# Token rows in SBUF at a pitch of 264 bytes instead of 256, in a long convolution by FFT with a token-mixing layer behind it

## The chip, the cores and the metric

The kernel runs on one core of a Trainium2 chip. The metric is the device time of one execution in microseconds. A profile comes from one execution; its times count from the first instruction of the program. Engines are called PE (matrix products; PEld is its loading of weights), DVE (vector), ACT (activation), POOL (general purpose, and the issuer of some DMAs) and SP (issuer of the other DMAs).

## What is computed

The input x has 8 batches of 5696 tokens with 128 channels. The first part convolves every channel of x with a filter h along the tokens, by FFT of double length; the second mixes tokens and channels.

```python
def _attn_ref(x, h):
    B, S, D = x.shape          # 8, 5696, 128
    L = 2 * S
    Xf = np.fft.rfft(x, n=L, axis=1)
    Hf = np.fft.rfft(h, n=L, axis=0)
    Yf = Xf * Hf[None, :, :]
    return np.fft.irfft(Yf, n=L, axis=1)[:, :S, :]

def _moe_ref(x, w_theta, w_tok_r, w_tok_i, w_ch):   # x: the result above
    theta = x @ w_theta
    zr, zi = x * np.cos(theta), x * np.sin(theta)
    y = einsum('ts,bsd->btd', w_tok_r, zr) + einsum('ts,bsd->btd', w_tok_i, zi)
    u = x + y
    return u + np.maximum(u @ w_ch, 0.0)
```

## The kernel before

**The FFT as matrix products.** The double length of 11392 is split as N1 x N2 = 178 x 64. A token number is 64 m + n, so the 5696 tokens are 89 rows m (NB = 89, on 89 partitions) of 64 columns n (N2). The forward transform has two stages, then comes the product with the transform of h, and two stages lead back:

- Stage A (`stage_a`, line 194) transforms along m. For one channel, the 89 x 128 block of x (two batches e, 64 columns n) is loaded into PE as weights, and the table f1_t (89 x 180: cosines and sines of 90 frequencies) is moved over it. Four channels make one chunk, which fills a PSUM tile and is emptied into the tile a (line 201, on ACT). A group has 64 channels, so 16 chunks.
- Stage B (`stage_b`, with `f2`, line 212) transforms along n, copies the result to SBUF (line 310, ACT) and multiplies it twice with tiles hs of the filter's transform (line 312, DVE) into u_t and v_t. hs is read from HBM by SP in 12 chunks per group, four chunks ahead.
- Stage C (`stage_c`, lines 328 and 329) and stage D (`stage_d`, line 351) transform back. C has 16 chunks of 16 matmuls; most of its results are emptied by DVE (line 336), some by ACT (lines 333, 334).

**Groups and their order.** There are eight groups: four pairs of batches (bp) times two halves of the channels (dh). PE takes its instructions in program order. In the loop at line 602, stage C of group g is woven with stage A of group g+1 (stage A first; it takes the first 0.35 of the stretch when g has the first half, 0.55 when it has the second), then stage B of group g+1 with stage D of group g. For the first group stage A runs alone (line 380).

**The loads of x.** `load_x` brings a pair of batches into the tile x16 of 128 x 2 x 64 x 128 float16 values, of which 89 partitions are used. The values are float32 in HBM and are converted by the DMA; such DMAs are issued by POOL. One load has 16 DMAs: two batches, four runs of 16 columns n, and partitions 0 to 79 and 80 to 88 apart. Within a partition a DMA's 16 columns of 128 channels lie in one run both in HBM (8 KB) and in SBUF (4 KB). The tile has one buffer, so the load of the next pair starts when the stage A that reads the second half is through (`next_x`, line 612, put at the end of that stage A's list). At most eight of these DMAs are under way at once; the ninth waits on the first.

The weights of one matmul in stage A are `x16[:NB, :, dh * HD + q]` with e and n merged: 128 columns at a step of one row of x16. The filter's own stage A, before all groups, reads `h16` in the same way, with rows of 64 values.

**What stands beside the loads.** POOL also makes the tables of sines and cosines (`turns_of`: an IOTA at line 150 and a product at line 152, then DVE at lines 155 and 156, then ACT); f2 needs the table w_t2 from there. The first x load is issued among these instructions. After the eight groups x16's room is given up and the mixing part follows: weights of 5696 x 5696 come in through a ring of buffers (line 509, POOL, converted from float32 by the DMA), are transposed by DVE (line 714) and multiplied on PE (line 1099).

Of the kernel before, what the change touches and what calls it, by code (L numbers as in the profile page):

```python
# [12 lines left out]
F16 = mybir.dt.float16  # L13
# [9 lines left out]
def kernel(  # L23
# [11 lines left out]
    B, S, D = x.shape  # L35
    assert D == 128
    P = 128
# [39 lines left out]
    N2 = 64  # L77
# [4 lines left out]
    HD = D // 2  # L82
    EN = N2 // 2 + 1
    WARM = 12
    assert N1 * N2 == NF and NB * N2 == S and NB % 2 == 1 and K1 <= P
    CHK = [(c0, min(CK, K1 - c0)) for c0 in range(0, K1, CK)]
    NCK = len(CHK)
# [14 lines left out]
    def pool(name, bufs, stack, **kw):  # L102
        return stack.enter_context(tc.tile_pool(name=name, bufs=bufs, **kw))
# [3 lines left out]
    fx = pool("fft_x", 1, xin)  # L107
# [11 lines left out]
    for p0, p1 in ((0, 80), (80, NB)):  # L119
        nc.gpsimd.dma_start(u_t[p0:p1, :N2 * D],  # L120
                            bass.AP(tensor=h.tensor, offset=h.offset + p0 * N2 * D,
                                    ap=[[N2 * D, p1 - p0], [1, N2 * D]]))

    def load_x(bp):
        x16 = fx.tile([P, 2, N2, D], F16, tag="x16", name="x16")
        for e in range(2):
            src = x[2 * bp + e]
            for n0 in range(0, N2, 16):
                for p0, p1 in ((0, 80), (80, NB)):
                    nc.gpsimd.dma_start(  # L130
                        x16[p0:p1, e, n0:n0 + 16, :].rearrange("p n d -> p (n d)"),
                        bass.AP(tensor=src.tensor, offset=src.offset + (p0 * N2 + n0) * D,
                                ap=[[N2 * D, p1 - p0], [1, 16 * D]]))
        return x16

    lane = fc.tile([P, 2], F32)
# [67 lines left out]
    def f2(a_st, c):  # L204
# [11 lines left out]
        if c == NCK - 1:  # L216
            for n in range(WARM):
                nc.tensor.matmul(ps[:, n % 2, ck * HD:ck * HD + 384], w_t2[:, 2, :P],
# [11 lines left out]
    for k0 in (0, 15, 30):  # L230
        w_table(k0)
    nc.vector.tensor_copy(h16[:NB], u_t[:NB, :N2 * D].rearrange("p (n h d) -> p h n d", h=2, d=HD))
    x16s = {0: load_x(0)}
    steps, a_h = stage_a(lambda q: h16[:NB].rearrange("p h n d -> p (h n) d")[:, :, q], True)
    woven(steps, [lambda k0=k0: w_table(k0) for k0 in range(45, K1, 15)])
# [366 lines left out]
    for g, (bp, dh) in enumerate(groups):  # L602
        st = {}
        last = g + 1 == len(groups)
        a_, load_, b_ = front(g + 1)
        if last:
            for _ in range(3):
                steps0.pop(0)()
        now = [with_load(steps0.pop(0), n < 6) for n in range(9)] if last else []
        c_ = stage_c(st, last)  # L610
        if dh == 0 and bp + 1 < B // 2:
            def next_x(bp=bp):
                x16s[bp + 1] = load_x(bp + 1)
            a_ = a_ + [next_x]
        woven((c_, 0.06 if a_ else 0.0, 1.0), (a_, 0.0, 0.35 if dh == 0 else 0.55), now, load_)
        if g + 2 == len(groups):
            xin.close()
            open_phases()
            load_ya0()
        now = [steps0.pop(0) for _ in range(5)] if last else []  # L620
        woven(b_, (stage_d(st, bp, dh, load_ya1 if last else None), 0.0, 1.1 if b_ else 1.0), now)
        if g + 2 == len(groups):
            load_ya1()
            open_ring()
# [537 lines left out]
```

## Time and profile before

| | us |
|---|---|
| three runs | 2100.75, 2101.3, 2103.45 |
| median | 2101.3 |
| span of the profiled execution, first to last instruction | 2098.1 |
| first matmul of stage A with x as weights | 54.5 |
| last one | 358.4 |
| the 512 matmuls of stage A: busy time on PE | 77.2 |
| mean of one of their weight loads | 0.241 |
| the four x loads begin (first issue on POOL) | 5.0, 100.0, 184.8, 270.1 |
| they have landed | 36.7, 118.3, 202.6, 289.6 |
| the stage A that needs them begins | 54.5, 128.8, 214.3, 301.0 |

The profile gives no time of its own for the profiled execution besides the span; the median of the runs is 3.2 us longer than the span.

How to read the lines that follow. In the list of costliest groups a line has the source line, the engine, the operation, what it writes and reads, shapes, the count, then busy time in us and mean of one in ns, then idle time before these instructions and what ended it. In the timeline a line has start and length in us, the engine, line and operation, and in brackets the idle time before it; several instructions in a row are merged (x12). In the DMA view a queue's line has packets, MB and the time that its packets took as a share of the 16 DMA engines; q0 carries what POOL issues, q1 what SP issues. The share can go over 100%, since a packet's time can overlap the next one's. In the 40 slices of the page each digit is the busy share in tenths, and PEclk the granted clock of PE in tenths of full speed. PE's matmuls are pipelined, so that their recorded lengths overlap; the distance between starts is the pace.

### The profile page before, as it was taken

The page shows a single profiled execution, that of the slowest core. Times are in us where ns is not written, and L with a number is a line of the kernel's source. Part 1 is how long each engine was busy: PE and PEld are TensorE (multiplying, and loading weights), DVE is VectorE, ACT ScalarE, POOL GpSimd, SP SyncE. Part 2 cuts the span into 40 slices and gives each one's busy share as a digit, 9 for nine tenths or more (in the row PEclk, how much of TensorE's full clock was granted, in tenths as well). Part 3 has the DMA queues.
Part 4 walks back from the last instruction along what each step waited for, and adds up shares of the span by engine and source line. Part 5 has one row for each costly group of instructions (what it writes and reads, how often), then busy time and mean ns, then how long its engine had stood idle before and what let it go on. Part 6 is the DMA issues. An engine that isn't in the chain of part 4 may idle for free.

```text
span 2098.1 us, 41505 instructions
## 1 busy us (share of the span) xinstructions
PE 1979.5 (94%) x15688; PEld 1109.4 (53%) x15865; DVE 1595.2 (76%) x2881; ACT 675.3 (32%) x995; POOL 912.5 (43%) x1662
## 2 busy tenths in 40 slices
PE   4888999878999999999999999899999999999998
PEld 3788888754444444444444444344444444444444
DVE  7777776776878888888886766886777777777867
ACT  5887877874332333333310000011111111111111
POOL 5301010327444636354557554435354545445450
PEclk8799999989999999999999999999999999999999
DMA  7357474989989989898999989869797887879693
GB/s 144 94 137 175 123 171 121 239 243 239 179 153 179 178 175 168 171 173 177 171 175 152 154 167 284 136 107 156 127 154 132 148 142 136 154 130 155 126 155 89
DMA packets 408233, 334.97 MB, mean 160 GB/s; under 512 B 85895, under 2 KB 358407, under 8 KB 407047
## 3 DMA queue, kind: packets, MB, share of 16 engines
q0 software_dynamic: 225952, 156.72, 52.8%
q1 hardware_dynamic: 176096, 164.05, 27.3%
q10 hardware_dynamic: 5984, 11.54, 1.6%
q8 instruction: 124, 2.03, 0.4%
q14 instruction: 77, 0.63, 0.1%
HBM read 377.11 MB, written 92.49 MB: 224 GB/s over the span
## 4 chain that ended last, share of the span: by engine, by line
PE 63%; DVE 4%; DMA 2%; issue 2%; POOL 0%; ACT 0%; DVEq 0%
PE m L1099 59%; DVE c L1106 2%; DMA ring<-in_moe_w_tok_r_dram 1%; DVE b L655 1%; PE v L801 1%; PE utp L794 1%; PE m L1103 1%; DVE wt L714 1%; PE tpz L742 0%; PE theta_ps L396 0%; POOL ring L509 0%; PE m L986 0%; DMA yT<-yt_hbm 0%; PE m L1020 0%; DMA zl<-zl_hbm 0%
## 5 line engine op out<-in xcount | busy, mean ns | idle before, releaser
L509 POOL DMA_DIRECT2D ring<-in_moe_w_tok_i_dram x720 | 390.8, 557 | 653.0 <-DVE wt L714 579.6
L509 POOL DMA_DIRECT2D ring<-in_moe_w_tok_r_dram x720 | 389.0, 559 | 145.8 <-DVE wt L714 85.5
L714 DVE STREAM_TRANSPOSE wt<-ring 128x384 f32<-128x384 f32 (+2 forms) x720 | 359.3, 523 | 110.3 <-PE m L1099 70.0
L1099 PE MATMUL m<-b,wt 128*128 128x512 bf16 x1599 | 385.9, 380 | 4.1 <-DVE wt L714 1.7
L1099 PEld LDWEIGHTS <-wt 128*128 128x128 bf16 x1804 | 176.4, 98 | 219.7 <-DVE wt L714 7.8
L1106 DVE TENSOR_TENSOR c<-c,m 128x512 f32<-128x512 f32 x412 | 265.2, 669 | 0.4 <-PE m L1099 0.4
L796 ACT ACTIVATE ring<-utp 128x512 bf16<-128x512 bf16 x85 | 50.8, 597 | 582.3 <-PE utp L794 582.3
L328 PE MATMUL ps<-r_u,u_t 128*128 128x128 f16 x1024 | 126.4, 223 | 6.4 <-ACT red L419 3.0
L329 PE MATMUL ps<-r_v,v_t 128*128 128x128 f16 x1024 | 125.5, 223 | 0.4
L1020 PE MATMUL m<-b,wt 128*128 128x512 bf16 x466 | 110.2, 381 | 8.9 <-DMA b<-z_hbm 4.9
L791 ACT ACTIVATE ub<-c 128x512 bf16<-128x512 f32 x88 | 55.0, 628 | 191.5 <-DMA ring<-in_moe_w_tok_r_dram 113.0
L130 POOL DMA_DIRECT2D x<-in_x_dram x64 | 33.9, 536 | 184.9 <-PE ps L194 174.8
L328 PEld LDWEIGHTS <-u_t 128*128 128x128 f16 x1024 | 103.4, 101 | 5.5 <-DVE u_t L312 4.6
L329 PEld LDWEIGHTS <-v_t 128*128 128x128 f16 x1024 | 102.4, 100 | 4.4 <-issue 2.4
L310 ACT ACTIVATE xs<-ps 128x1024 f16<-128x1024 f32 x96 | 96.6, 1030 | 14.7 <-DVE v_t L312 6.7
L312 DVE TENSOR_TENSOR u_t<-xs,hs 128x1024 f16<-128x1024 f16 x96 | 68.6, 715 | 29.2 <-ACT xs L310 19.0
L1020 PEld LDWEIGHTS <-wt 128*128 128x128 bf16 x528 | 51.1, 99 | 69.2 <-issue 9.6
L194 PE MATMUL ps<-f_t,x 89*128 89x180 f16 x512 | 77.2, 298 | 4.0 <-ACT xs L310 2.6
L212 PEld LDWEIGHTS <-w_t 64*128 64x128 f16 x3240 | 60.8, 102 | 37.5 <-issue 24.5
L398 ACT ACTIVATE red<-theta_ps,magic 128x512 f32<-128x512 f32 (+1 forms) x46 | 31.6, 687 | 134.6 <-PE theta_ps L396 104.5
L194 PEld LDWEIGHTS <-x 89*128 89x128 f16 x512 | 70.8, 241 | 5.5 <-issue 4.5
L744 ACT ACTIVATE ring<-tpz 128x512 bf16<-128x512 bf16 (+1 forms) x46 | 27.5, 597 | 131.9 <-PE tpz L742 113.0
(2895 smaller groups left out, 3868.9 us busy)
## 6 DMA issues: line engine op xcount, KB each, us to landing
ring<-in_moe_w_tok_r_dram POOLq DMA_DIRECT2D x352, 96.0 KB, 4.5
ring<-in_moe_w_tok_i_dram POOLq DMA_DIRECT2D x352, 96.0 KB, 4.9
ring<-in_moe_w_tok_r_dram POOLq DMA_DIRECT2D x352, 80.0 KB, 4.5
ring<-in_moe_w_tok_i_dram POOLq DMA_DIRECT2D x352, 80.0 KB, 3.9
hs<-hf_hbm SPq DMA_DIRECT2D x192, 128.0 KB, 3.1
cp_hbm<-c SPq DMA_DIRECT2D x88, 256.0 KB, 2.5
c<-cp_hbm SPq DMA_DIRECT2D x88, 256.0 KB, 4.4
out_dram<-c SPq DMA_DIRECT2D x88, 256.0 KB, 4.5
```

The source lines that it names most:

```text
L194: nc.tensor.matmul(ps[:, i // 2, (i % 2) * 2 * K1:(i % 2 + 1) * 2 * K1], lhs(q + i), f1_t[:NB], start=True, stop=True)
L212: nc.tensor.matmul(ps[:, e, j * HD:(j + 1) * HD], w_t2[rows, c0 + j, N2 * (1 - ri):N2 * (3 - ri)], a_st["a"][rows, ri * K1 + c0 + j, :], s ...
L310: nc.scalar.activation(xs[:, :, :, :ck], ps, AF.Copy)
L312: nc.vector.tensor_tensor(uv[r][:, :, :, c0:c0 + ck], xs[:, :, :, :ck], hv[:, r:r + 1, :, :ck].to_broadcast([P, 2, HD, ck]), op=mult)
L328: nc.tensor.matmul(o, u_t[:, at:at + P], r_u, start=True, stop=False)
L329: nc.tensor.matmul(o, v_t[:, at:at + P], r_v, start=False, stop=True)
L509: nc.gpsimd.dma_start(wb[32 * i:32 * i + 32, :ng, :nj * 64], bass.AP(tensor=a.tensor, offset=a.offset + row0 * S + p * H + i * QR + j0 * 6 ...
L714: nc.vector.transpose(wt.rearrange("p j t r -> p (j t r)").bitcast(F32).rearrange("p (j g t) -> p g j t", j=TJ, g=4)[:, :ng, :nj], wb[:, : ...
L791: nc.scalar.activation(ub[:m].rearrange("p b d -> p (b d)"), c[:m], AF.Copy)
L1020: nc.tensor.matmul(ms[n // 2 * 2 + h], a[n][:, j, :, r], bts_of[p][jj][n % 2 * 2 + h][:, r, :], start=(n % 2 == 0 and jj == 0 and r == 0), ...
L1099: nc.tensor.matmul(ms[q], a[q][:, j, :, r], bts[jj][q][:, r, :], start=(jj == 0 and r == 0), stop=(jj == NJ - 1 and r == 1 and q not in left))
L1106: nc.vector.tensor_tensor(c, z, ms[q], op=op)
```

## The change

The rows of x16 get a pitch XP = D + 4 = 132 values (264 bytes) instead of 128 (256 bytes); the four values at the end of each row are neither written nor read. The loads name the 128 values of each row, so the SBUF side of a DMA is no longer one run per partition, and the HBM side is written with the row as a dimension of its own. What is moved, and all matmuls, stay as they are; only the step between the columns of stage A's weights differs. The tile takes 33,792 bytes per partition instead of 32,768.

```diff
     WARM = 12
+    XP = D + 4
...
     def load_x(bp):
-        x16 = fx.tile([P, 2, N2, D], F16, tag="x16", name="x16")
+        x16 = fx.tile([P, 2, N2, XP], F16, tag="x16", name="x16")
         for e in range(2):
             src = x[2 * bp + e]
             for n0 in range(0, N2, 16):
                 for p0, p1 in ((0, 80), (80, NB)):
                     nc.gpsimd.dma_start(
-                        x16[p0:p1, e, n0:n0 + 16, :].rearrange("p n d -> p (n d)"),
+                        x16[p0:p1, e, n0:n0 + 16, :D],
                         bass.AP(tensor=src.tensor, offset=src.offset + (p0 * N2 + n0) * D,
-                                ap=[[N2 * D, p1 - p0], [1, 16 * D]]))
+                                ap=[[N2 * D, p1 - p0], [D, 16], [1, D]]))
         return x16
```

## The prediction

> **What bounds the kernel.** I read the page's engine table first, then its 40 slices, then the chain. PE is busy for 94% of the span and the chain lies on PE for 63% of it, almost all of that in a line of the later mixing part; the change touches only the first 360 us.
>
> ```profile
> PE 1979.5 (94%) x15688; PEld 1109.4 (53%) x15865; DVE 1595.2 (76%) x2881; ACT 675.3 (32%) x995; POOL 912.5 (43%) x1662
> ...
> PEclk8799999989999999999999999999999999999999
> DMA  7357474989989989898999989869797887879693
> ...
> L194 PE MATMUL ps<-f_t,x 89*128 89x180 f16 x512 | 77.2, 298 | 4.0 <-ACT xs L310 2.6
> ```
>
> The stages follow one another on PE in program order, so I count a microsecond won or lost before 360 us as one at the end. The last line, from the costliest groups, shows where: stage A, 512 matmuls with x as weights, fills 77 us of PE.
>
> **The intended gain: the weight read.** Stage A against its neighbour, stage C, in the timeline:
>
> ```profile
> 131.42 0.22 PE L328 MATMUL ps<-r_u,u_t 128*128 128x128 f16 x1
> 131.48 0.22 PE L329 MATMUL ps<-r_v,v_t 128*128 128x128 f16 x1
> ```
> ```profile
> 92.97 1.57 PEld L194 LDWEIGHTS <-x 89*128 89x128 f16 x12
> ```
>
> Stage C, 128 columns moved over contiguous weights, starts a matmul every 0.055 us. By columns stage A's 180 would take 0.055 x 180/128 = 77 ns. But its twelve weight loads took 1.57 us, the last of them about 0.24 (the page's mean), so 1.33/11 = 121 ns from start to start. So at full clock stage A is paced by its weight loads, 44 ns over its matmul. At half clock a matmul needs twice 77 ns and nothing is to be won.
>
> Whether 264 bytes read faster than 256 no row shows. The nearest are loads in stretches at half clock (from 88.8 to 92.0 us, and h from 16 to 19):
>
> ```profile
> L194 PEld LDWEIGHTS <-x 89*128 89x128 f16 x10 | 1.5, 207 | 0.0
> L328 PEld LDWEIGHTS <-u_t 128*128 128x128 f16 x9 | 1.3, 140 | 0.0
> ```
> ```profile
> L194 PEld LDWEIGHTS <-h 89*128 89x128 f16 x21 | 3.2, 172 | 0.0
> ```
>
> Contiguous weights (u_t) take 140 ns, h16 with a column step of 128 bytes 172, x16 with 256 bytes 207. So the step matters. Two readings fit: farther steps simply cost more (then 264 costs what 256 does), or powers of two return to the same part of the memory (then 8 bytes more may help a little or much). By nearness 264 is next to 256, and 8 bytes leave neighbouring columns almost where they were modulo 256. I take **no gain**, and keep both ends. Upper end of the gain: group 0's stage A gives nothing, since ACT empties PSUM back to back there (16 evictions in 10.79 us, 0.67 each, against 4 x 0.121 = 0.48 on PE). For the other 448 matmuls, some 85% of which the timeline has at full clock, 44 ns is 448 x 0.044 x 0.85 = 16.8 us, 2.4 per group; ACT's idle time before these evictions was only 1.7 to 2.3 us per group, so I count 1.9 x 7 = **13 us**. Lower end: if the longer step cost as much again as that from 128 to 256 bytes, 35 ns, it would be 448 x 0.035 x 0.85 = 13 us of loss.
>
> The Trainium skill ("SBUF — State Buffer", Specifications (TRN2)) says that full bandwidth needs two accesses or more to a 16-byte line and that each crossing to a new line pays. By it 128, 256 and 264 bytes are all the same, since every column is a new line, and the gain is nothing. The rows agree that strided weights are slower, but not that all strides are equal (172 against 207).
>
> **The price: the loads of x.** One x load is 16 DMAs (eight of 80 partitions, eight of 9), issued by POOL, which convert from float32. Today a partition's 16 rows are one run of 4 KB in SBUF. With gaps of 8 bytes they become 16 runs of 256 bytes: 712 pieces per load become 712 x 16 = 11,392. On this queue pieces of converting DMAs are not joined: the weight ring's 768- and 640-byte rows appear one packet each. Rates, from the DMA view of four stretches (packets, MB, share of 16 engines): 102 to 114 us (x), 1050 to 1052 (640-byte rows), and the two kinds of 1053 to 1058 (128-byte rows beside other traffic):
>
> ```profile
> q0 software_dynamic: 836, 2.39, 104.1%
> ```
> ```profile
> q0 software_dynamic: 665, 0.38, 133.3%
> ```
> ```profile
> q0 software_dynamic: 1595, 0.21, 63.3%
> q1 hardware_dynamic: 806, 0.72, 50.8%
> ```
>
> Now: 836 packets less 252 that only signal are 584 in 12 us, so 712 take 14.6 us. The 640-byte rows: 665 less 73 are 592 in 2 us on 16 engines, 54 ns each. The 128-byte rows: 0.633 x 5 x 16 / 1595 = 31.7 ns, over a total share of 1.14, so 28 ns of service. A 256-byte piece lies a quarter of the way: 28 + 26/4 = **34 ns** (ends: 28 and 54). A load is then 11,392 x 34/16 = 24.2 us instead of 14.6 (ends: 19.9 and 38.5).
>
> Is there room? The x16 buffer is single, so a load starts when the second half's stage A has read it, and must land before the next pair's stage A:
>
> ```profile
> 100.00 4.25 POOL L130 DMA_DIRECT2D x<-in_x_dram  x8 [27.41 <-PE ps L194]
> ```
> ```profile
> 128.76 1.94 PE L194 MATMUL ps<-f_t,x 89*128 89x180 f16 x12
> ```
> ```profile
> q0 software_dynamic: 1024, 2.92, 54.5%
> q1 hardware_dynamic: 1345, 2.21, 27.4%
> q8 instruction: 5, 0.08, 1.1%
> ```
>
> The window is 100.0 to 128.7; the last of x lands at 118.3 today (issues and landings of the timeline), 10.4 us early. The last fence is the DMA view of this window: besides x the engines carry 27.4% of 28.7 = 7.9 us of hs (the filter tiles) and 0.3 of instructions. After a lead-in of some 1.3 us they have 27.4 us; they would need 24.2 + 7.9 + 0.3 = 32.4. So x is **5.0 us late**, and PE, which takes its instructions in order, stands before stage A with stage C's matmuls queued behind. The 0.7 us or so of landing and the half microsecond that PE idles there now (0.36 before the first C matmul) cancel. The windows of the loads at 184.8 and 270.1 are alike (landings at 202.6 and 289.6 before matmuls at 214.3 and 301.0): 3 x 5 = 15 us. Which loses, x or hs, matters little: late hs holds DVE's multiplication, which comes before the same point.
>
> POOL's own part: the 512-piece DMAs of line 542 took 802 ns, the 80-piece ones 531, so 271/432 = 0.63 ns per piece and 1200 x 0.63 = 0.75 us more per large DMA. For the later loads it is covered: 8 x 1.28 + 8 x 0.56 = 14.7 us of issue beside 24 us of transfer. In the first load it stands ahead of the tables:
>
> ```profile
> 23.03 6.16 POOL L130 DMA_DIRECT2D x<-in_x_dram  x11
> 29.19 1.97 POOL L150 IOTA whole<- 128x960 f32 x2
> 31.26 2.22 POOL L152 TENSOR_SCALAR turn<-whole,lane 128x960 f32<-128x960 f32 x2
> ```
>
> Six large ones from 21 us on move this by 4.5 us; the first of the two L152 then ends at 36.9 instead of 32.4, and DVE, which took it at 35.86, is **1.0 us** late, with the tables for which PE waits. The two large ones before fall into POOL's wait of 9.42 us at 20.10. The first load's transfer (landed by 36.7, needed at 54.5) has 18 us of room and needs 10 more. One KB more of SBUF per partition costs no time.
>
> The Trainium skill ("DMA: Bandwidth & Descriptors", Why small descriptors are slow) gives a 256-byte piece 8 data cycles and 3 of overhead. By that estimate a load would take 14.6 x 11/8 = 20.1 us, nearly in time, and the change would cost 2 to 4 us. The rows above (a fifth of the bytes for half the time) say more.
>
> **Sum.** 1.0 + 15 + 0 = +16 us on a span of 2098.1. The page gives no other time for the profiled execution; the median of the runs, 2101.3, lies 3.2 above its span, and I add the same: 2098.1 + 16 + 3.2 = 2117.3.
>
> **Rivals.**
> 1. *The read becomes fast and x still lands in time* (piece near 28 ns, or a better spread over the engines): -13 + 1 = -12, 2089. For: 172 against 207 at half and whole step, and 10.4 us of slack today. Against: both must hold. It decides from a piece below 28 ns.
> 2. *Fast read, late x*: -13 + 16 = +3, 2104 (2092 to 2115).
> 3. *The pitch does not do what it says and x lands in time*: +1 to +3, 2103.
> 4. *The read gets slower*: +13 + 16, 2130.
>
> **Numbers.** Chances: forecast 0.42, rivals 0.16, 0.18, 0.17, 0.07. Forecast's own range: 1 + 3 x 0.7 gives 2104 at 28 ns a piece, and 45 ns (32.0 us a load, 12.8 late) gives 2141; 54 ns would be 2160. The range from 2092 to 2141 leaves out most of rival 1 and the far ends. By 0.2% (4.2 us, about what a measurement can tell from no change): faster is rival 1 and a quarter of 2, 0.21; the same is most of 3, half of 2 and the forecast's lowest end, 0.25; slower is the rest, 0.54.
>
> **What would show it.** Right: about 46,000 packets more on q0; stage A's weight loads still near 121 ns apart and 207 long at half clock; x landing 130 to 135 us instead of 118, with PE idle before L194 on the DMA of x three times; the L130 issues near 1.3 us. Wrong: weight loads under 90 ns apart, joined packets on q0 (then no lateness at all), or x landing before 128 us.

## The result, and the profile after

The changed kernel takes 2090.7 us (median of four runs, 2088.3 to 2092.4) against 2101.2 for the kernel before, run beside it: a ratio of 0.9946, interval 0.9931 to 0.9960. It is 11 us faster, where I had forecast 16 us slower. The profiled execution took 2088.3 us with a span of 2086.5 (before: 2098.1).

The engine table and two rows of the 40 slices, of the changed kernel:

```profile
PE 1968.8 (94%) x15865; PEld 1085.1 (52%) x15865; DVE 1579.1 (76%) x2881; ACT 659.4 (32%) x995; POOL 915.7 (44%) x1662
...
PEclk8799989999999999999999999999999999999999
DMA  9489595989898989898999899869697878878793
```

PE still carries the span, with 11 us less of busy time. The granted clock shows one thing that I had not asked about: the sixth slice, 261 to 313 us, has 8 here and 9 before. The cause comes below.

**The weight read became fast.** The view of stage A's line, before and then after (min/median/max in ns, first and last start in us, the shape):

```profile
L194 PEld LDWEIGHTS <-x x512: 202/238/310, 54.2 to 358.2; 89*128 89x128 f16 x171
L194 PE MATMUL ps<-f_t,x x512: 237/292/406, 54.5 to 358.4; 89*128 89x180 f16 x171
```
```profile
L195 PEld LDWEIGHTS <-x x512: 149/157/188, 56.8 to 347.9; 89*128 89x128 f16 x171
L195 PE MATMUL ps<-f_t,x x512: 237/241/359, 56.9 to 348.0; 89*128 89x180 f16 x171
```

The median weight load fell from 238 to 157 ns. What counts is the pace, read from the timeline as in the prediction:

```profile
91.94 1.01 PEld L195 LDWEIGHTS <-x 89*128 89x128 f16 x12
```

Twelve loads in 1.01 us, the last of them about 0.157: (1.01 - 0.157)/11 = 78 ns from start to start, where it was 121. That is the 77 ns that the 180 columns need, so weight loads no longer pace stage A.

**The pieces came as forecast, and moved faster.** The DMA view from the issue of the second x load to the stage A that needs it (97.9 to 130.1 us):

```profile
q0 software_dynamic: 12544, 2.92, 95.4%
q1 hardware_dynamic: 1351, 2.22, 26.9%
q8 instruction: 5, 0.08, 1.0%
```

The load is 12,544 packets instead of 1024, for the same 2.92 MB. Its last piece lands at 123.05 us, 7 us ahead of the need:

```profile
97.92 7.56 POOL L131 DMA_DIRECT2D x<-in_x_dram  x10 [24.58 <-PE ps L195]
```
```profile
130.13 1.14 PE L195 MATMUL ps<-f_t,x 89*128 89x180 f16 x12
```

**Where the time went.** A period is the time from one group's stage A to the next one's. The loads of x fall between groups 1 and 2, 3 and 4, 5 and 6. All in us, from the first matmuls of stage A in the traces:

| | before | changed |
|---|---|---|
| stage A of group 0 begins | 54.5 | 56.9 |
| period from group 0 | 30.0 | 29.4 |
| periods with an x load (from groups 1, 3, 5) | 44.2, 45.2, 46.2 | 43.8, 46.7, 47.8 |
| periods without (from groups 2, 4, 6) | 40.3, 40.5, 40.1 | 36.9, 36.5, 36.5 |
| stage A of group 7 | 17.3 | 13.6 |

A period without an x load keeps a gain of 3.4 to 4.0 us. One with a load keeps 0.4 or loses 1.5, although its stage A is just as much shorter (first to last matmul: 14.9, 15.1, 14.7 before, 11.1, 11.2, 11.3 after). All eight stages A together became 25.6 us shorter. The pieces took back 2.4 at the start and, in the three periods, 3.4, 5.4 and 5.0 us of what stage A had won, 13.8 in all. That makes -9 of the -11.6 in the span; the rest lies scattered in the other periods and behind stage A. The experiments first price the two halves and then ask how pieces that land in time can cost that much.

### The profile page after: what moved, and what is told of

The parts are those of the page before. It is cut to its first block, busy times and chain, and to the rows that moved or that the text cites. A ratio compares the mean times of both kernels' runs of the same rounds, so it can differ in the third digit from the quotient of the medians.

```text
span 2086.5 us, 41684 instructions
## 1 busy us (share of the span) xinstructions
PE 1968.8 (94%) x15865; PEld 1085.1 (52%) x15865; DVE 1579.1 (76%) x2881; ACT 659.4 (32%) x995; POOL 915.7 (44%) x1662
## 4 chain that ended last, share of the span: by engine, by line
PE 64%; DVE 3%; DMA 3%; issue 1%; POOL 1%; ACT 0%; DVEq 0%; POOLq 0%
PE m L1100 60%; DMA ring<-in_moe_w_tok_r_dram 2%; DVE c L1107 1%; POOL ring L510 1%; PE v L802 1%; PE utp L795 1%; PE m L1104 1%; DVE b L656 1%; DVE wt L715 1%; PE theta_ps L397 0%; PE tpz L743 0%; PE m L987 0%; PE m L1021 0%; DMA ring<-in_moe_w_tok_i_dram 0%; DMA zl<-zl_hbm 0%
## 5 line engine op out<-in xcount | busy, mean ns | idle before, releaser
L131 POOL DMA_DIRECT2D x<-in_x_dram x64 | 48.5, 764 | 169.1 <-PE ps L195 159.5
L311 ACT ACTIVATE xs<-ps 128x1024 f16<-128x1024 f32 x96 | 91.8, 984 | 19.4 <-PE ps L213 5.2
L421 ACT ACTIVATE mag<-mag,half_pi 128x512 f32<-128x512 f32 (+1 forms) x90 | 65.6, 729 | 0.0
L313 DVE TENSOR_TENSOR v_t<-xs,hs 128x1024 f16<-128x1024 f16 x96 | 63.5, 662 | 0.0
```

Source lines behind the costliest of these rows:

```text
L311: nc.scalar.activation(xs[:, :, :, :ck], ps, AF.Copy)
L313: nc.vector.tensor_tensor(uv[r][:, :, :, c0:c0 + ck], xs[:, :, :, :ck], hv[:, r:r + 1, :, :ck].to_broadcast([P, 2, HD, ck]), op=mult)
L421: nc.scalar.activation(mag, mag, AF.Sin, bias=half_pi[:m], scale=-TWO_PI)
```

## The experiments

All times are compared with the kernel before, run beside each one.

### The pieces alone: pitch 128, each DMA takes every fourth row

```diff
-    x16[p0:p1, e, n0:n0 + 16, :].rearrange("p n d -> p (n d)"),
+    x16[:, e].rearrange("p (k j) d -> p j k d", j=4)[p0:p1, n0 // 16],
...
-            ap=[[N2 * D, p1 - p0], [1, 16 * D]]))
+            ap=[[N2 * D, p1 - p0], [4 * D, 16], [1, D]]))
```

> The pitch stays at 128 values, but each DMA of the load takes every fourth row, so that its runs in SBUF are 256 bytes long as in the changed kernel: the small pieces without the new column step. Theory (the change is a gain of about 25 us in stage A, less about 14 us in the three stretches in which x is loaded and 2 us at the start): 2115 to 2118 us, weight loads as before (about 240 ns), the periods that hold an x load 4 to 5 us longer than before, the others as before. Rival (the small pieces cost nearly nothing, and the rest of stage A's gain is lost because ACT or DVE become the bound of the weave): 2101 to 2104 us.

Measured: 2119.5 us against 2101.7, ratio 1.0088 (1.0073 to 1.0103). The pieces alone cost 18 us, a little more than I had expected. The three periods with a load take 51.1, 51.5 and 51.5 us; those without stay at 40.

### The pitch alone: rows of 132 values, filled as unbroken runs

```diff
-    x16[p0:p1, e, n0:n0 + 16, :D],
+    x16[:, e].rearrange("p n d -> p (n d)")[p0:p1, n0 * XP:(n0 + 16) * XP],
...
```

The DMAs bring 2112 values in one run, so what stands in x16 is shifted against the rows.

> Weights are read at a step of 132 values, but the loads are written in runs of 2112 values without gaps, so the values in x16 are shifted against the right ones (the result is another one; work and times are the same): the new step without small pieces. Theory: 2075 to 2079 us (2101 less 25), stage A's matmuls 78 ns apart, each period shorter by 3 to 4 us. Rival (ACT or DVE limit the weave): 2087 to 2091 us, as in the changed kernel.

Measured: 2077.6 us, ratio 0.9889 (0.9870 to 0.9907), 24 us faster. Its weight loads are those of the changed kernel:

```profile
L195 PEld LDWEIGHTS <-x x512: 150/157/189, 53.7 to 334.5; 89*128 89x128 f16 x171
```

So both halves of the change act, with opposite signs. They don't quite add up: -24 and +18 make -6, and the change measured -11. With the fast read the same pieces cost 13 us (2090.7 against 2077.6). Why the slow read makes them dearer was not tried.

### Other pitches: 129, 130, 136 and 144 values

One pitch for each of the four x loads (258, 260, 272 and 288 bytes), with the same 256-byte pieces.

```diff
-    XP = D + 4
+    PITCH = (129, 130, 136, 144)
...
+        XP = PITCH[bp]
```

> The changed kernel with another pitch for each of the four x loads: 129, 130, 136 and 144 values (258, 260, 272, 288 bytes). If the step of 256 bytes is bad because it returns to the same place in a period of the memory that is a power of two, all four are about as fast as 132 (matmuls 78 ns apart, weight loads below 170 ns). If 8-byte steps were what counts, 129 and 130 would be slow (120 ns apart); if the loads get better the farther apart the columns are modulo 256 bytes, 144 has the shortest weight loads and 129 the longest.

Measured: 2091.8 us in one run, as the changed kernel. The median weight load (138, 152, 144 and 144 ns) and the pace of 77 to 78 ns hardly depend on the pitch. The line's view:

```profile
L198 PEld LDWEIGHTS <-x x512: 135/144/183, 57.7 to 348.2; 89*128 89x128 f16 x171
```

### Steps below 256 bytes: 64, 96, 112 and 124 values

Pitch 128 and unbroken runs as before; the weights are read from x16 at 128, 192, 224 and 248 bytes, so that other values are multiplied.

```diff
+    STEP = (64, 96, 112, 124)
...
+        steps, a_st = stage_a(lambda q: x16[:NB, dh * HD + q:dh * HD + q + 128 * st_].rearrange(
+            "p (c d) -> p c d", d=st_)[:, :, 0])
```

> The kernel before, with weights read from the same tile at steps of 64, 96, 112 and 124 values (128, 192, 224, 248 bytes) for the four pairs, so that other values than the right ones are multiplied: the weight read alone at other steps. If the cost grows with the step, all four lie between contiguous (98 ns) and 256 bytes (about 240 ns) in this order, 248 bytes being nearly as slow as 256. If powers of two are bad, 128 bytes is the slowest of the four (matmuls more than 80 ns apart), 192 between, and 224 and 248 are as fast as 264 (78 ns apart, about 157 ns).

Measured: 2072.7 us in one run. Together with the runs above, median weight load and pace of stage A in ns:

| column step, bytes | 128 | 192 | 224 | 248 | 256 | 258 | 260 | 264 | 272 | 288 |
|---|---|---|---|---|---|---|---|---|---|---|
| weight load | 177-183 | 141 | 142 | 157 | 238 | 138 | 152 | 157 | 144 | 144 |
| pace | 92-96 | 77-78 | 78 | 78 | 121 | 77-78 | 77-78 | 78 | 77-78 | 77-78 |

Distance isn't it: 248 and 258 bytes, on both sides of 256, are fast. The two slow steps are the powers of two. They are also the only multiples of 128 bytes here; a step of 384, which would tell these two readings apart, was not tried. The Trainium skill ("SBUF — State Buffer", Specifications (TRN2)) lets each crossing of a 16-byte line pay; all ten steps cross a line at every column, so by that rule alone they would be equal, and the measured 138 to 238 ns contradict that.

### Is it hs that comes late? Six buffers of hs instead of four

The changed kernel shows DVE waiting for hs, the filter tiles that share the DMA engines with x. Waits of DVE from the stage A of group 1 to that of group 6 (us in total, times, longest), before and after:

```profile
DVE u_t L312 <- DMA hs<-hf_hbm: 4.6, 7, 1.2
```
```profile
DVE u_t L313 <- DMA hs<-hf_hbm: 11.6, 8, 3.3
```

This was my first theory. The test gives hs two more buffers and two chunks more lead:

```diff
+    fh2 = pool("fft_h2", 2, xin)
...
-    def stage_b(a_st, dh):
+    def stage_b(a_st, dh, deep):
+        LEAD = 6 if deep else 4
...
-            hs = hs_of[c] = fh.tile([P, 2, HD * CK], F16, tag="hs", name="hs")
+            hs = hs_of[c] = (fh2 if deep and c % 6 > 3 else fh).tile([P, 2, HD * CK], F16, tag="hs", name="hs")
```

> The changed kernel with six filter tiles hs fetched ahead instead of four (two more buffers beside x16, for all groups but the last). Theory (what the small pieces cost later is that hs comes late to stage B while x is still loading): stage B can start two chunks, some 3.5 us, farther before it needs a late tile; most of the 3.4 to 5.4 us lost in each of the three periods with an x load comes back: 2079 to 2084 us. Rival (the loss lies elsewhere, for instance in POOL's issue or in memory contention with DVE and ACT): 2089 to 2092 us.

The same with the old pitch, as a control:

> The same two additional hs buffers in the kernel before, as the control: stage B waits there for hs only 6.5 us in all, so both theories expect 2096 to 2102 us.

Measured: 2088.2 us (ratio 0.9930, 0.9912 to 0.9949), only 2.5 better than the changed kernel, while the control alone won 6 us (2097.0 against 2103.3, ratio 0.9968, 0.9955 to 0.9980). With six buffers DVE's waits for hs are gone from those periods, yet the periods with a load still take 45.0, 45.7 and 47.5 us. **My theory fell**: late hs is not the cause.

### What waits instead: TensorE's own instructions

What did not go is a wait that the profile calls "issue": PE waits for nothing that it shows. PE's waits from the stage A of group 1 to that of group 6, of the kernel before, the changed kernel, the six buffers and the pitch alone:

```profile
PE ps L212 <- issue: 7.5, 5, 2.7
PE ps L351 <- ACT xs L310: 3.1, 6, 1.8
...
PE ps L351 <- issue: 0.5, 1, 0.5
```
```profile
PE ps L213 <- issue: 10.8, 6, 4.2
PE ps L352 <- issue: 5.2, 3, 4.1
```
```profile
PE ps L214 <- issue: 10.3, 5, 4.0
PE ps L355 <- issue: 5.3, 2, 3.9
```
```profile
PE ps L213 <- issue: 6.2, 5, 2.6
PE ps L352 <- ACT xs L311: 3.4, 7, 1.8
...
PE ps L352 <- issue: 0.8, 1, 0.8
```

8 us before, 16 in the changed kernel with four buffers of hs or six, 7 with the pitch alone; 17 with the pieces alone. Before and with the pitch alone one stop of 1.8 us each, the longest in the ACT lines, stands at a place where the changed kernel has a stop called issue (520 in the table of places below). Counted by place, the sums are 10 before, 16 in the changed kernel and 9 with the pitch alone. The stops stand in the periods with a load. Each meets one 16 KB packet on queue 8, the one that the DMA view calls "instruction":

```profile
q8 instruction: 124, 2.03, 0.4%
```

This is the changed kernel's page: 124 packets of 16,384 bytes. PE has 2 x 15,865 = 31,730 instructions, 256 for each packet. The Trainium skill ("Runtime: NRT & Kernel Launch", Instruction fetch mechanics) says the same of the size, blocks of 16 KB with 256 instructions fetched through a DMA queue, and that the fetch is mostly hidden. The runs here agree on the block and show 16 us that are not hidden.

In the trace PE starts again 2.3 to 3.1 us after the packet has begun, before, with the pitch alone and after alike; what differs is when it begins. For the load of group 5's period the packet begins at 287.2 us before (PE stands from 287.0 to 289.7), at 270.1 with the pitch alone (271.9 to 273.1) and at 281.2 in the changed kernel (279.7 to 283.9): there 1.6 us after PE has run dry.

That the x pieces make it late shows when the three packets for the ends at 499, 520 and 541 are timed from the end of the block before, 128 matmuls earlier. They begin 2.4, 1.9 and 3.7 us after it before, 2.9, 2.1 and 1.7 us with the pitch alone, but 3.3, 4.0 and 5.1 us in the changed kernel and 3.2, 4.1 and 4.8 us with the pieces alone. Where no other packet has started since that end or in the microsecond ahead of it, such a packet begins at most 0.7 us after the end (105 packets, all runs).

The clock makes long stops dearer. The changed kernel around that stop, then the pitch alone around its own: a stretch in us, its length, busy time and count of PE, PEld, DVE, ACT and POOL, then PEclk, DMA share and GB/s:

```profile
277.00:279.70 2.70, 2.67 (x98) 2.36 (x95) 2.50 (x4) 2.70 (x4) 0.19 (x1) 1.00 2.51 156
279.70:283.90 4.20, 0.00 (x0) 0.00 (x0) 1.29 (x2) 1.87 (x3) 0.00 (x0) 0.77 1.68 168
283.90:288.90 5.00, 4.98 (x124) 4.67 (x125) 3.12 (x5) 3.27 (x4) 0.00 (x0) 0.50 1.08 211
288.90:293.90 5.00, 4.09 (x94) 3.67 (x92) 2.64 (x6) 3.27 (x4) 0.00 (x0) 0.50 0.54 170
```
```profile
271.90:273.00 1.10, 0.03 (x1) 0.00 (x0) 0.96 (x2) 1.09 (x2) 0.00 (x0) 1.00 0.72 217
273.00:278.00 5.00, 4.17 (x175) 3.81 (x176) 4.15 (x8) 4.41 (x6) 0.00 (x0) 1.00 0.69 199
278.00:283.00 5.00, 3.97 (x108) 3.01 (x101) 4.28 (x8) 4.82 (x6) 0.00 (x0) 1.00 0.52 166
```

After 4.2 us without a matmul PE gets half its clock for ten microseconds, and 124 matmuls start in the next 5 us where 175 do after a stop of 1.1 us, which leaves the clock whole. Over the three periods with a load, the changed kernel takes 138.2 us and the pitch alone 126.5. The stops, counted by place, account for 7 of the 12 us more (16.0 against 8.8), the lower clock goes with 6.5 us more of PE's busy time (115.1 against 108.6); together that is more than 12, since other waits of PE became shorter.

### Do the stops belong to the instructions' blocks? 64 small matmuls more

```diff
+    ps = psum()
+    for n in range(64):
+        nc.tensor.matmul(ps[:, 0, :8], f1_t[:NB, :P], f1_t[:NB, :8], start=True, stop=True)
```

> The changed kernel with 64 small matmuls (128 TensorE instructions, 8 columns each, result never read) ahead of the first transform of h, where TensorE waits for data until 15.0 us. Theory (TensorE's instructions come in blocks of 16 KB, 256 of them, over the DMA engines, and the 3.6 to 4.2 us stops at L213 and L352 in the periods with an x load are such blocks coming late): every block now ends 128 instructions earlier in the program, so the stops stand at other matmuls, about 64 before or after the old places; the time changes by what the new places are worth, 2086 to 2095 us. Rival (those matmuls wait for something in the program that the profile doesn't name): the stops stay at the same matmuls of the same chunks, and the time at 2091.

The place of each stop over 0.9 us after the first 20 matmuls of its group, counted in matmuls from the start of the group's stage A:

| kernel | from group 1 | from group 3 | from group 5 |
|---|---|---|---|
| before | 499 | 520, 648, 776 | 541 |
| changed | 499, 627 | 520, 648 | 541, 669 |
| changed, run again (below) | 499, 627 | 520, 648 | 541 |
| pieces alone | 499, 627 | 520 | 541, 669 |
| pitch alone | 499 | 520 | 541 |
| 64 matmuls more | 435, 563 | 456, 584 | 477, 605 |

Within a period the stops lie 128 or 256 matmuls apart, and with 64 matmuls more ahead they come exactly 64 earlier in each of the three periods, at other operations of the program. A wait of the program's own would have stayed with its instruction. So the stops are the ends of instruction blocks. The time was 2096.7 us (ratio 0.9973, 0.9960 to 0.9986), a little past the range that I had given. The three periods with a load take 144.4 us (138.2 in the changed kernel): the stops called issue sum to 16.7 us (16.0), the longest 5.0, and PE's busy time to 117.6 (115.1); what the rest is was not taken apart.

### How small is small? Pieces of 512 bytes at the old pitch

```diff
+    x16[:, e].rearrange("p (k j r) d -> p j k (r d)", j=4, r=2)[p0:p1, n0 // 16],
...
+            ap=[[N2 * D, p1 - p0], [8 * D, 8], [1, 2 * D]]))
```

> The kernel before (pitch 128) with x loaded in pieces of 512 bytes, two rows each: half as many pieces as in the changed kernel, and the old weight read. Theory (the loss follows from how long the x load occupies the DMA engines: 14.6 us in runs of 4 KB, about 18.5 in pieces of 256 bytes): pieces of 512 bytes would take about 16 us, so that a third of the 18 us that the small pieces alone cost is left: 2105 to 2110 us. Rival (the cost comes with any cut of the run, for instance through the descriptors on POOL): 2113 us or more.

Measured: 2109.0 us, ratio 1.0040 (1.0026 to 1.0055): 6 us dearer than before by the medians, 8 by the ratio, within the range. Half as many pieces cost a third to a half of the 18 us; the longest stops are 3.0, 2.6 and 3.2 us, between those of before (2.2, 1.8, 2.7) and of the pieces alone (3.3, 4.4, 4.3).

### Can the pieces be kept out of the way? Two half tiles

x16 becomes two tiles of 64 channels at a pitch of 72 values. Each can be loaded as soon as its own stage A is through, so that a half load falls into nearly every period; the pieces shrink to 128 bytes.

```diff
-            x16 = fx.tile([P, 2, N2, XP], F16, tag="x16", name="x16")
+            x16s[bp, dh] = fx.tile([P, 2, N2, XP], F16, tag=f"x16_{dh}", name="x16")
...
+                x16s[bp, dh][p0:p1, e, n0:n0 + 16, :HD],
```

> x in two tiles of 64 channels each, at a pitch of 72 values (144 bytes), in pieces of 128 bytes; each half is loaded again as soon as its own stage A has read it, with the DMAs spread over stages C, B and D of that group, not in one burst. Theory (the whole loss is the burst of x before stage B): all of stage A's gain is kept, 2076 to 2081 us. Rival (the number of pieces counts, wherever they lie; here twice as many): 2095 us or more.

Measured: 2086.5 us, ratio 0.9923 (0.9906 to 0.9941). The five periods from group 2 to 7 take 199.0 us together, as with the pitch alone (198.6; the changed kernel 204.3), although twice as many pieces move. But the period from group 1 takes 49.4 us, for the third half load runs from 70 to 97 us, beside the hs of that period. Two runs tried to move it, the first with a copy that waits for the middle of the next group's stage A:

```diff
+            a_.insert(8, lambda: nc.gpsimd.tensor_copy(gate[:, 0:1], sts[g + 1]["a"][:, 0, HD // 2 - 1:HD // 2]))
```

> Half-channel tiles as in the half-tile run before, but each half load is held back (GpSimd first copies one element that the middle of the next group's first transform has written) so that its pieces move in the period just before the group that reads them, and the second load no longer moves at 70 to 97 us. Theory (what the small pieces cost in the changed kernel is the late fetch of TensorE's instructions behind them and the half clock after it; a half load per period, half as long a burst, leaves that no room): the five later periods stay at 199 us together as in the run before, the one that held 49.4 us comes down to 41 to 43, so 2078 to 2081 us. Rival (half tiles in twice as many 128-byte pieces cost as much wherever they are put): 2084 to 2088, as before.

Here 12 of its 16 DMAs had been issued before the hold, since nothing tied them to it: 2084.2 us (0.9918, 0.9901 to 0.9936), and the period takes 49.5 us as before. It tested nothing. The second writes into the half tile itself:

```diff
+                if after is not None:
+                    nc.gpsimd.tensor_copy(x16s[bp, dh][:, :, 0:N2:16, 0],
+                                          sts[after]["a"][:, 0:8, HD - 1].rearrange("p (e n) -> p e n", e=2))
```

> As the run before with the hold, which held only 4 of the 16 transfers of the second load: now GpSimd's copy writes an element into every part of the half tile that the transfers then overwrite, so that none of them can start before the next group's first transform has ended. Theory (small pieces cost through what they delay while they move: hs and TensorE's instructions): nothing of x moves at 70 to 97 us any more, the 49.5 us period falls to 41 to 44 and the five after it stay at 199 us together, so 2077 to 2082 us. Rival (the stall at 83 to 94 us isn't from the load, or moves with it): 2084 to 2088, as in the two runs before.

Measured: 2087.1 us (0.9941, 0.9921 to 0.9961). Half of the expectation held: that period fell from 49.5 to 41.1 us. The five after it rose from 199.0 to 207.9, with stops of PE as long as 3.4 us:

```profile
PE ps L219 <- issue: 8.2, 7, 2.6
PE ps L359 <- issue: 6.1, 3, 3.4
```

14 us over these five periods, against 10 in the first version with half tiles. What a burst costs depends on where the end of an instruction block falls in it, and I can't say ahead where that is. The changed kernel itself, run again beside this one:

> The changed kernel again, beside the run above on the same chip, for their difference: 2089 to 2093 us.

Measured: 2088.9 us, ratio 0.9945 (0.9928 to 0.9962), a shade below the range. Its periods with a load take 46.9, 47.1 and 46.6 us, where the first profile had 43.8, 46.7 and 47.8: the stops keep their places, but their lengths differ from run to run. Of the versions that compute the right result, the half tiles are at best some 5 us better than the change, and their intervals touch its own.

## Why the prediction was wrong, point by point

- **"By nearness 264 is next to 256 ... I take no gain."** This step failed. I had named both readings, and the bound that decides was in my hands: 121 against 77 ns. But I took the distance in bytes as the measure of nearness, with h at 128 bytes as the only other step, and that is itself a power of two. The runs show 248 and 258 bytes about as fast as 192. The term was -25.6 us of stage A instead of 0.
- **The upper end of the gain, 13 us, was too small as well.** I capped it by ACT's idle time, 1.7 to 2.3 us per group. I had read that in two groups; over groups 1 to 7 it is 1.6 to 3.2, 15.7 together instead of 13. Besides that idle time, 20 of ACT's 128 evictions in stage A were themselves long, over 1.15 us. One group, before and after (min/median/max in ns):

```profile
L201 ACT ACTIVATE a__2375<-ps x16: 771/824/1317, 130.2 to 145.3; 128x720 f16<-128x720 f32 x16
```
```profile
L202 ACT ACTIVATE a__2375<-ps x16: 765/770/802, 130.7 to 143.3; 128x720 f16<-128x720 f32 x16
```

  All of the long ones are gone with the faster read. In groups 1 to 7 the evictions sum to 97.8 us before and 87.2 after, 1.5 less per group, and ACT's idle time before them fell from 15.7 to 6.8, 1.3 less per group. That is 19.5 of the 25.4 us by which these seven stages became shorter; the rest was not taken apart. Stage A now goes at about ACT's pace (16 x 0.775 = 12.4 us of evictions in most groups). A busy time in the profile can hold a wait, as these long evictions seem to.
- **The pieces: the number was right, the price was not.** 46,080 packets more on q0 (forecast 46,000). In the stretch from 100.0 to 118.4 us, DMA view of the changed kernel:

```profile
q0 software_dynamic: 12024, 2.81, 160.7%
q1 hardware_dynamic: 168, 0.28, 8.3%
```

  16 engines x 18.4 us / 12,024 = 24.5 ns of an engine for a packet, with some hs beside it, instead of my 34 (ends 28 and 54). Each packet's recorded time is 16 x 18.4 x 1.607 / 12,024 = 39 ns, but they overlap. I had allowed for that at 128 bytes and then added too much for the size. So x lands at 123 us, not at 130 to 135, and PE never waits on it; by this sign, which I had named, the mechanism of the loss was wrong. Part of the margin comes from the fast read: the load starts 11.6 us into the period instead of 15.5. But with the pieces alone, whose read is as slow as I forecast, x also lands in time (130.5 us, needed at 138.4), and the loss is 18 us all the same.
- **"3 x 5 = 15 us", and "which loses, x or hs, matters little".** The size was near, 13.8 us, for another reason. I counted hs and 0.3 us of instructions as load on the engines and asked only whether all of it fits into the window. It fits. But an instruction block is needed at a point in the middle of the burst. There its packet begins 0.5 to 1.6 us after PE has run dry, PE stands for 3.6 to 4.2 us, and a lower clock follows. The line `q8 instruction: 5, 0.08, 1.1%` stood in my own fence.
- **POOL's issue: 0.90 us for a large x DMA** (median in the trace; all 64 together, `x64 | 48.5, 764`), where I had 1.28. Its effect on the first load was larger all the same. POOL in the changed kernel:

```profile
24.11 7.73 POOL L131 DMA_DIRECT2D x<-in_x_dram  x10
32.97 1.50 POOL L131 DMA_DIRECT2D x<-in_x_dram  x2 [1.14 <-DMA x<-in_x_dram]
34.48 1.97 POOL L151 IOTA whole<- 128x960 f32 x2
36.55 2.68 POOL L153 TENSOR_SCALAR turn<-whole,lane 128x960 f32<-128x960 f32 x2
```

  The slower transfers make POOL wait 1.14 us for the limit of eight under way, which I had left out. DVE takes the first table at 37.64 instead of 35.86, 1.8 us late (forecast 1.0), and group 0's stage A begins 2.4 us later.
- **The rivals.** The time is that of the first rival, 2089: a fast read with x in time. Its condition, a piece below 28 ns, holds too. But it reached the figure with a gain of 13 and a price of 1; the runs show 25 and 16 (2.4 + 13.8). Two errors of about the same size cancelled: that the time is this rival's is luck. The second rival, a fast read and a loss of 16, has the loss right in size, but not its cause, since x is not late.

## What to carry to other kernels

When weights are read at a column step of 128 or 256 bytes and the matmuls start farther apart than their columns take, try a few elements of padding: here each of the eight steps tried from 192 to 288 bytes, 256 itself apart, brought PE to its own pace. Then price what the padding does to the loads, and not only whether they land in time: small pieces also hold up PE's instructions, which come over the same DMA engines, so a stop called "issue" that sits at multiples of 128 matmuls beside a burst of DMA is a late block. A stop of 2.4 us or more cost twice here, once by itself and once by the clock after it; one of 1.4 to 2.2 us mostly did.

## What the runs showed of the hardware

- Weight loads of 128 columns of float16: 238 ns at a step of 256 bytes, 177 to 183 at 128, 138 to 157 at the eight other steps from 192 to 288.
- Between 95 and 350 us the traces of all runs hold 30 stops of PE of 2.4 to 5.0 us that began at full clock. After every one the granted clock of the next 5 us was lower, 0.50 to 0.66. Of 20 stops of 1.4 to 2.2 us 16 were followed by 0.57 to 0.68 (one of 1.7 us in the changed kernel, at 206.1, by 0.66) and four by 1.00 (1.6, 1.8, 1.8 and 2.2 us), so the length alone doesn't decide there. In the clock records each stretch at one level lasts a multiple of 3.41 us; whether a stop's place against that grid decides was not tested. The Trainium skill ("TensorE: Matmul & The Clock Gate", HAM oscillation) sets the bound at gaps of some 3.4 us; here shorter ones sufficed.
- PE needs a new block of 256 instructions every 128 matmuls. In stage B, where 25 matmuls take 0.54 us in the timeline, a block lasts so short a time that a packet which begins 0.5 to 1.6 us after PE has run dry means a stop of 3.6 to 4.2 us.
